# Accumulating transfers inside the product sums of a spectral filter, with finer loads and a new order

## The chip, the cores and the metric

One core of one Trainium2 chip runs the whole program. The metric is the device time of one execution in microseconds (us). Times inside the program are counted from the start of the profiled span.

## The reference

Two layers, the same twice; x is 2048 tokens by 448 features in bf16:

```python
def _A_ref(x, w_r, w_i):                     # W has 2048 x 225 entries
    X = rfft2(x.astype(float32), axes=(-2, -1)) * (w_r + 1j * w_i)
    return irfft2(X, s=(2048, 448), axes=(-2, -1)).astype(bfloat16)

def _B_ref(x, w1, b1, w2, b2):               # 448 -> 1792 -> 448
    h = relu(x @ w1 + b1)
    return (h * h) @ w2 + b2

x = x + _A_ref(_layernorm(x), A_w_r, A_w_i)
x = x + _B_ref(_layernorm(x), B_w1, B_b1, B_w2, B_b2)
x = x + _A_ref(_layernorm(x), A_w_r, A_w_i)
x = x + _B_ref(_layernorm(x), B_w1, B_b1, B_w2, B_b2)
```

## The kernel before

All stages keep their data in SBUF. Tokens lie as 16 tiles of 128 (xin for the input, x_sb for the running sum). A layer has these stages:

- **A** (A1 in layer 1, A2 in layer 2, mixed into the end of layer 1's FFN): layer norm statistics and the first short transform over tokens, 16 tiles, to XA.
- **spectral** (line 1140): for each of the items, a pair p of frequency groups (1 to 7, and 0 for the two groups that stand alone), **TD** (line 809, the transform over features, two halves a pair, each with an evacuation to U), **B** (line 820, the second transform over tokens with the matrices G, evacuated to EF), **W** (line 861, the filter) on VectorE, and **Bi** (line 903, the inverse with H or HS), evacuated to VT.
- **TI, AI** (lines 937 to 1001): the inverse transforms over features and tokens, added to x_sb; **ln** (line 1018): the second layer norm and a transposed copy yT.
- **h, o** (lines 1058 to 1122): the FFN.

W works on pairs (2,3), (4,5), (6,7) two at a time, and on 1 and 0 alone. For a pair it takes E and F (in layer 1, except pair 1, first their sum T0 and T1), multiplies them with the filter rows and their mirror image (two products, T2 to T5), and then goes one of two ways. For pairs 4 to 7 (the tuple SUMS) two sums give Z and Bi sums the rest itself, with four matmuls of 512 columns a half. For pairs 1 to 3 two sums give T6 and T7 and two more give Z, and Bi takes four matmuls of 256 columns a half. With `n=2` a sum has 896 elements a partition and a product 1792; with `n=1`, half of that.

Filter rows come from DRAM to Wt. Their mirror image (token frequency -k) is gathered by GpSimd to Wm, which lies in the memory of yT, and copied reversed from there to Wt by two transfers on SP's queue.

The order of all work is written out. Each instruction is first recorded with its dependences (from the memory it reads and writes), grouped in units that carry a tag; the table ORDER gives a rank to each unit of a tag, with a letter where the engine is chosen (a ScalarE, d VectorE, p GpSimd) and after a colon its PSUM banks. `ranked` and `schedule` (lines 392 and 413) sort all units by rank; each engine and each DMA queue then runs its own in that order, and waits only on semaphores. A DMA also waits until the one 20 places ahead of it on SP's queue is through. WARM puts matmuls without use at the start. The numbers in `cost` and `lat` are the planner's and do nothing on the chip.

## Time and profile before

| what | us |
|---|---|
| median of 3 runs (266.8 to 268.77) | 267.41 |
| the profiled execution | 267.51 |
| its span, first to last instruction | 265.7 |
| TensorE busy with matmuls | 256.0 |
| VectorE busy | 211.5 |
| ScalarE busy | 171.7 |
| GpSimd busy | 9.9 |

The profile is one execution. Its own time and its span differ by 1.8 us that lie before the first and after the last instruction. A busy TensorE may still be waiting between matmuls, since these are pipelined and their ends are modelled: where a rate matters, starts of rows are compared. The granted TensorE clock is 1.0 of full speed throughout.

### The profile page before, as it was taken

To read this page: it belongs to the slowest core of one execution; us is meant where nothing else is said; L and a number is where in the kernel's file an instruction comes from. 1 tells how busy PE (TensorE), PEld (TensorE's weight loads), DVE (VectorE), ACT (ScalarE), POOL (GpSimd) and SP (SyncE) were. 2 spreads that over 40 slices of the span, in tenths; PEclk is the share of its full clock that TensorE was granted. 3 is DMA by queue.
4 is the path that set the end of the run, shared out by engine and by line. 5 is a ranking of instruction groups with operands and counts; after the bars stand their busy time and mean duration, and the time that the engine had idled before them with its cause. 6 is when DMAs were issued, how large, how long until landed. Compare 5 with 4: busy or idle time off the path is not lost. (4 is left out here: it accounts for less than half of the span.)

```text
span 265.7 us, 5784 instructions
## 1 busy us (share of the span) xinstructions
PE 256.0 (96%) x2188; PEld 161.6 (61%) x2190; DVE 211.5 (80%) x646; ACT 171.7 (65%) x392; POOL 9.9 (4%) x30
## 2 busy tenths in 40 slices
...
GB/s 235 273 318 209 158 293 220 2 39 42 75 2 0 41 73 62 20 0 0 2 0 4 2 2 0 2 41 4 41 74 42 0 57 133 53 4 0 72 39 48
DMA packets 29423, 17.82 MB, mean 67 GB/s; under 512 B 22066, under 2 KB 28306, under 8 KB 29268
## 3 DMA queue, kind: packets, MB, share of 16 engines
...
q10 hardware_dynamic: 432, 0.69, 0.8%
...
q14 instruction: 10, 0.08, 0.1%
...
## 5 line engine op out<-in xcount | busy, mean ns | idle before, releaser
L556 PE MATMUL ps<-yT,W_sb 64*128 64x512 bf16 (+1 forms) x770 | 90.2, 346 | 0.0
L556 PE MATMUL ps<-W_sb,arena 128*128 128x448 bf16 (+2 forms) x490 | 87.3, 336 | 0.0
L556 PEld LDWEIGHTS ps<-yT,W_sb 64*128 64x128 bf16 (+1 forms) x770 | 55.0, 95 | 32.0 <-issue 1.5
L556 PEld LDWEIGHTS ps<-W_sb,arena 128*128 128x128 bf16 x490 | 46.2, 98 | 36.6 <-DVE arena L608 0.9
L575 ACT ACTIVATE arena<-ps,b1col 128x512 bf16<-128x512 f32 x84 | 51.8, 692 | 14.6 <-PE ps L556 14.5
L608 DVE TENSOR_TENSOR arena<-arena 128x512 bf16<-128x512 bf16 (+1 forms) x140 | 45.2, 369 | 17.2 <-ACT arena L575 16.8
L581 ACT ACTIVATE arena<-ps 128x448 bf16<-128x448 f32 (+1 forms) x42 | 24.5, 686 | 3.5 <-PE ps L556 3.4
L1120 DVE SCALAR_TENSOR_TENSOR x_sb<-ps,arena 128x448 bf16<-128x448 f32 (+2 forms) x27 | 15.2, 570 | 14.4 <-PE ps L556 14.3
L1024 ACT ACTIVATE VT<-x_sb 128x448 bf16<-128x448 bf16 x32 | 18.5, 581 | 12.3 <-DVE x_sb L1000 12.3
L575 ACT ACTIVATE arena<-ps 128x256 bf16<-128x256 f32 x56 | 18.0, 396 | 6.3 <-PE ps L556 6.2
L575 ACT ACTIVATE mv<-mv,epst 128x1 f32<-128x1 f32 (+1 forms) x45 | 12.6, 296 | 14.2 <-DVE rstd L715 7.3
L581 ACT ACTIVATE VT<-ps 128x512 bf16<-128x512 f32 (+1 forms) x28 | 13.9, 578 | 6.7 <-PE ps L556 6.6
L556 PE MATMUL ps<-yT,VT 64*128 64x512 bf16 x42 | 15.8, 376 | 0.0
L581 ACT ACTIVATE XA<-ps 128x512 bf16<-128x512 f32 x27 | 14.5, 593 | 1.0 <-PE ps L556 1.0
L556 PE MATMUL ps<-HS_sb,arena 128*128 128x512 bf16 x62 | 14.7, 380 | 0.2
L556 PE MATMUL ps<-arena,G_sb 128*128 128x448 bf16 (+1 forms) x76 | 14.4, 333 | 0.1
L556 PE MATMUL ps<-TD_sb,XA 112*64 112x112 bf16 (+2 forms) x312 | 13.4, 224 | 0.0
L556 PEld LDWEIGHTS ps<-TD_sb,XA 112*64 112x64 bf16 (+2 forms) x312 | 12.1, 108 | 1.3 <-issue 0.4
L608 DVE TENSOR_TENSOR tmp<-arena,Wt 128x896 bf16<-128x896 bf16 (+1 forms) x14 | 10.9, 820 | 1.9 <-DMA Wt<-yT 1.8
L592 ACT ACTIVATE arena<-x_sb,rstd 128x448 bf16<-128x448 bf16 x10 | 6.6, 667 | 8.9 <-DMA yT<-arena 4.6
L556 PE MATMUL ps<-x_sb,xin 128*128 128x256 bf16 x64 | 8.9, 272 | 3.1 <-ACT x_sb L592 1.8
L1050 DVE SCALAR_TENSOR_TENSOR arena<-x_sb,mv,b2row 128x448 bf16<-128x448 bf16 x16 | 10.7, 681 | 0.1
...
## 6 DMA issues: line engine op xcount, KB each, us to landing
...
G_sb<-c_G SPq DMA_DIRECT2D x1, 960.0 KB, 7.9
xin<-in_A_x_dram SPq DMA_DIRECT2D x4, 224.0 KB
Wt<-yT SPq DMA_DIRECT2D x2, 392.0 KB, 8.7
xin<-in_A_x_dram ACTq DMA_DIRECT2D x3, 224.0 KB, 3.3
```

The costliest lines, as they stand in the source:

```text
L556: return sch.add("pe", lambda e: e.matmul(_res(o), lhsT, rhs, start=start, stop=stop, skip_group_check=skip), [lhsT, rhs], [o], cost=cost, ...
L575: sch.add("act", lambda e: e.activation(o, _res(i), func, **kw), rd, [o], cost=c)
L581: op = sch.add(engs[0], lambda e: e.activation(o, _res(i), ACT.Copy) if h[0].eng == "act" else e.tensor_copy(o, _res(i)), [i], [o], cost=c ...
L592: op = sch.add(engs[0], lambda e: e.activation(o, i, ACT.Copy, scale=s) if h[0].eng == "act" else e.tensor_scalar(o, i, s, 1.0, op0=ALU.mu ...
L608: sch.add(eng, lambda e: e.tensor_tensor(o, _res(a), b, op), [a, b], [o], cost=_free(o) / rate + 69.0)
L1024: sch.add("act", lambda e, i=i, o=o, x=x: e.activation(o, x, ACT.Square, accum_out=mv[:, i, 4:5]), [x], [o, mv[:, i, 4:5]], cost=560.0)
L1050: small(lambda e, o=o, x=x, m=m: e.scalar_tensor_tensor(out=o, in0=x, scalar=m, in1=b2row[:], op0=ALU.add, op1=ALU.add), [x, m, b2row[:]], ...
L1120: small(lambda e: e.scalar_tensor_tensor(out=o, in0=_res(i), scalar=r[0] if r else 1.0, in1=xb[:, t, d0:d1], op0=ALU.mult, op1=ALU.add), [ ...
```

## The change

- The last two sums of pairs 2 and 3 (in both layers) and of pair 1 (in layer 2) are no longer formed from T6 and T7: a transfer from SBUF to SBUF, issued by GpSimd, adds products T4, T5 onto T2, T3 (`dma_add`). One product is made with negated filter rows so that the difference is a sum; GpSimd or ScalarE negates them once a layer, into W2_sb (layer 1) or xin (layer 2). Two sums on VectorE (tag V) then give Z.
- Pairs 4 and 5 go the same way, and so leave SUMS: Bi takes matmuls of 256 columns for them. Pairs 6 and 7 stay.
- The products get two or three scratch areas: tmp, tmp2 (in yT, over Wm), and tmp3 (in xin).
- Filter, G and W2 are loaded in more pieces and in another order, from input tile 5 instead of 7 on; W2's first nine blocks come after layer 1's filter. J is loaded late.
- b1 is loaded in rows and turned by a matmul with J.
- ORDER is new throughout, and layer 2 takes its pairs in the order 6, 7, 2, 3, 4, 5, 1, 0. There are 15 matmuls of WARM instead of 12.

The core of the diff; of ORDER only the new lines that are spoken of:

```diff
--- before.py
+++ after.py
...
-SUMS = {True: (4, 5, 6, 7), False: (4, 5, 6, 7)}
+ADDS = {True: (2, 4), False: (1, 2, 4)}
+ADD_LAT = 4500.0
+ITEMS = {True: (1, 2, 3, 4, 5, 6, 7, 0), False: (6, 7, 2, 3, 4, 5, 1, 0)}
+SUMS = {True: (6, 7), False: (6, 7)}
...
+    "dve.arena": "28", "sp.TD_sb": "54", "sp.G_sb": "21 25 18 24",
+    "sp.Wt": "22 26 19 16 73 61 69 60 20 17 71 62 23 51", "sp.H_sb": "211 200", "sp.HS_sb": "182", "sp.TI_sb": "70",
+    "sp.J_sb": "253", "sp.FI_sb": "196", "sp.b2row": "241", "sp.b1in": "166", "b1": "286:6 290d",
+    "sp.W1_sb": "218 207 234 262", "sp.W2_sb": "156 276", "A1.0": "29 30 34 35 31p 67p 81:2 108a",
+    "A1.14": "97 110 98 103 112 120 111p 121p 138:5 154a 122a 141:7 146d", "NA1": "171p 184p 213p 223p",
+    "TD0.1": "153:6 172d 161:0 169a", "B0.1": "185:6 193a 189:0 197a", "W0.1": "195 205 206 209 228 231",
+    "B0.3": "168:4 178d", "W0.3": "180 181 186 190 194", "V0.3": "242 244", "TD0.4": "177:7 183a 176:3 187a",
+    "W0.5": "212 210 225 217 227", "V0.5": "263 261", "TD0.6": "219:2 220a 221:1 224a", "B0.6": "229:4 230a",
+    "TD0.7": "204:0 216a 214:3 215a", "B0.7": "222:6 226a", "W0.7": "236 239 250 246 255 257", "TD0.0": "232:2 233a",
+    "B0.0": "237:6 243a", "W0.0": "267 269 272 273", "Bi0.1": "238:1 251a 235:0 240a",
+    "W1.7": "901 906 916 910", "TD1.2": "875:4 878a 903:2 904a", "B1.2": "912:3 918a 909:2 913a",
+    "TD1.3": "895:4 899d 897:5 902a", "B1.3": "905:0 911a", "W1.3": "925 919 931", "V1.3": "954 957",
+    "B1.5": "915:4 921a", "W1.5": "930 932 938", "V1.5": "963 964", "TD1.1": "882:4 891d 927:7 928a",
+    "B1.1": "929:6 935d 933:7 936a", "W1.1": "939 937 942", "V1.1": "969 970", "TD1.0": "924:0 934a",
+    "B1.0": "940:4 943a", "W1.0": "950 945 951 948", "Bi1.6": "949:3 955a 947:2 978d",
...
-WARM = {46: ((7, 512), (7, 512), (7, 512), (7, 512), (7, 512), (7, 512), (7, 512), (7, 512), (7, 512), (7, 512), (7,
-    512), (7, 512))}
+WARM = {64: ((7, 512), (7, 512), (7, 512), (7, 512), (7, 512), (7, 512), (7, 512), (7, 512), (7, 512), (7, 512), (7,
+    512), (7, 512), (7, 512), (7, 512), (7, 512))}
...
-        xin = sb("xin", [P, NT, D])
+        xw = sb("xw", [P, NT * D + 32 * LW + FB * D])
+        xin = xw[:, 0:NT * D].rearrange("p (t d) -> p t d", t=NT)
+        Wt = xw[:, NT * D:NT * D + 32 * LW].rearrange("p (q l) -> p q l", q=32)
+        W2_sb = xw[:, NT * D + 32 * LW:].rearrange("p (f d) -> p f d", f=FB)
...
-        Wt = sb("Wt", [P, 32, LW])
+        tmp2 = yT[:].rearrange("p a b c -> p (a b c)")[:, 0:8 * 4 * LW].rearrange("p (a b c d) -> p a b c d", a=8, b=2, c=2)
+        tmp3 = xin[:, 9:15, :].rearrange("p a (b c d) -> p a b c d", b=1, c=2)
...
+        def dma_add(o, i):
+            sch.add("pool", lambda e: e.dma_start(o, i, accum_op=ALU.add), [o, i], [o], is_dma=True, cost=1000.0, lat=ADD_LAT)
...
-        for i in range(2):
-            dma("sp", Wp[:, :, 3 - 2 * i, :], Wm[:, i, :].rearrange("p (k l) -> p k l", k=7)[:, ::-1, 1:225])
         memset(Z[:, :, LW:256], 0.0)
-        x4 = [xin[:, 7, :]]
-        dma("sp", J_sb[:], dc["J"], after=x4)
+        x4 = [xin[:, 5, :]]
+        w_dram = [w.rearrange("(p k) l -> p k l", k=16) for w in (A_w_r, A_w_i)]
+
+        def load_W(p0, p1):
+            for i in range(2):
+                tagged("sp.Wt", "sp", Wp[:, p0 - 1:p1 - 1, 2 * i, :], w_dram[i][:, p0:p1, 1:225], after=x4)
+
+        def mirror_W(p0, p1):
+            for i in range(2):
+                m = Wm[:, i, :].rearrange("p (k l) -> p k l", k=7)[:, ::-1, 1:225]
+                tagged("sp.Wt", "sp", Wp[:, p0 - 1:p1 - 1, 3 - 2 * i, :], m[:, p0 - 1:p1 - 1])
+
+        def load_G(c0, c1):
+            dma("sp", G_sb[:, c0:c1], dc["G"][:, c0:c1], after=x4)
+
         dma("sp", TD_sb[:], dc["TD"], after=x4)
-
-        w_dram = [w.rearrange("(p k) l -> p k l", k=16) for w in (A_w_r, A_w_i)]
-        dma("sp", G_sb[:, 6:], dc["G"][:, 6:], after=x4)
-        for i in range(2):
-            dma("sp", Wp[:, :, 2 * i, :], w_dram[i][:, 1:8, 1:225], after=x4)
+        load_G(6, 12)
+        load_W(1, 2)
+        load_G(12, 20)
+        load_W(2, 4)
+        mirror_W(1, 2)
+        load_G(20, cst["G"].shape[1])
+        mirror_W(2, 4)
+        load_W(4, 8)
+        mirror_W(4, 8)
         if H_PAIRS:
             dma("sp", H_sb[:, 2:], dc["H"][:, 2:], after=x4)
+        load_G(0, 6)
+        for i in range(2):
+            tagged("sp.Wt", "sp", W08[:, :, i, :], w_dram[i][:, 0:9:8, 1:225], after=x4)
+        dma("sp", H_sb[:, 0:2], dc["H"][:, 0:2], after=x4)
         dma("sp", HS_sb[:], dc["HS"][:, SD_PAIRS[0] - 1:SD_PAIRS[-1]], after=x4)
-        dma("sp", G_sb[:, 0:6], dc["G"][:, 0:6], after=x4)
-        dma("sp", H_sb[:, 0:2], dc["H"][:, 0:2], after=x4)
-        for i in range(2):
-            dma("sp", W08[:, :, i, :], w_dram[i][:, 0:9:8, 1:225], after=x4)
         dma("sp", TI_sb[:], dc["TI"], after=x4)
+        dma("sp", J_sb[:], dc["J"], after=x4)
         dma("sp", FI_sb[:], dc["FI"], after=x4)
         dma("sp", b2row[:], B_b2.partition_broadcast(P), after=x4)
-        dma("sp", b1in[:, 0:FB], B_b1.rearrange("(fb fl) -> fl fb", fl=P), after=x4)
-        cp(b1col[:, 0:FB], b1in[:, 0:FB])
+        dma("sp", b1in[0:FB, :], B_b1.rearrange("(fb fl) -> fb fl", fl=P), after=x4)
+        sch.tag = "b1"
+        q = _Tile(1)
+        mm(q[lambda b: ps[:, b, 0:FB]], b1in[0:FB, :], J_sb[0:FB, P - 1:P - FB - 1:-1], True, True)
+        evac(b1col[:, 0:FB], q[lambda b: ps[:, b, 0:FB]])
+        sch.tag = ""
         dma("sp", W1_sb[:, 0:3, :], B_w1[0:384, :].rearrange("(b p) f -> p b f", p=P), after=x4)
         dma("sp", W1_sb[0:64, 3, :], B_w1[384:448, :], after=x4)
-        dma("sp", W2_sb[:], B_w2.rearrange("(fb fl) d -> fl fb d", fl=P), after=x4)
-
+        w2 = B_w2.rearrange("(fb fl) d -> fl fb d", fl=P)
+        tagged("sp.W2_sb", "sp", W2_sb[:, 9:], w2[:, 9:], after=x4)
         for r in (64, 65):
             dma("sp", W1_sb[r:r + 1, 3, :], B_b1.rearrange("(o f) -> o f", o=1), after=x4)
...
+        def negate(first):
+            sch.tag = "NA1" if first else "NA2"
+            for p0 in ADDS[first]:
+                for q in range(p0 - 1, p0 + (p0 > 1)):
+                    o, i = (W2_sb if first else xin)[:, 2 * q, :], Wp[:, q, 0:2, :].rearrange("p s l -> p (s l)")
+                    negate_one(o, i)
+
+        def negate_one(o, i):
+            h = []
+            op = sch.add("pool", lambda e: e.activation(o, i, ACT.Copy, scale=-1.0) if h[0].eng == "act" else
+                         e.tensor_scalar(o, i, -1.0, 1.0, op0=ALU.mult, op1=ALU.mult), [i], [o], cost=640.0)
+            h.append(op)
+            op.alt = {"pool": 640.0, "act": 470.0}
+
         def stage_W(p0, n, first):
             z_ = Z[:, :, 0:LW]
             if p0 > 0:
                 ef = EF[:, 2 * p0:2 * (p0 + n), :].rearrange("p (q e) (r l) -> p q e r l", e=2, r=2)
                 E, F = ef[:, :, 0], ef[:, :, 1]
-                T = [tmp[:, i, 0:n] for i in range(8)]
+                tm = (tmp2 if p0 in (2, 6) else tmp) if first else {6: tmp, 2: tmp2, 4: tmp, 1: tmp3}[p0]
+                T = [tm[:, i, 0:n] for i in range(6 if tm is tmp3 else 8)]
                 w = Wp[:, p0 - 1:p0 - 1 + n].rearrange("p q (a r) l -> p a q (r l)", a=2)
                 if p0 in (VB_PAIRS if first else V_PAIRS):
                     T[0:2] = E, F
                 else:
                     tt(T[0], E, F[:, :, ::-1, :], ALU.subtract)
                     tt(T[1], E[:, :, ::-1, :], F, ALU.add)
-                for i, wi in enumerate((w, w[:, ::-1])):
+                add = p0 in ADDS[first]
+                w0 = w
+                if add:
+                    x = (W2_sb if first else xin)[:, 2 * (p0 - 1):2 * (p0 + n) - 3:2, :]
+                    w0 = bass.AP(x.tensor, x.offset, [list(x.ap[0]), [w[:, 1].offset - x.offset, 2], [4 * LW, n], [1, 2 * LW]])
+                for i, wi in enumerate((w0, w[:, ::-1])):
                     t = T[i].rearrange("p q r l -> p q (r l)")[:, None].to_broadcast([P, 2, n, 2 * LW])
-                    tt(tmp[:, 2 + i:5 + i:2, 0:n].rearrange("p a q r l -> p a q (r l)"), t, wi, ALU.mult)
+                    tt(tm[:, 2 + 2 * i:4 + 2 * i, 0:n].rearrange("p a q r l -> p a q (r l)"), t, wi, ALU.mult)
                 z = z_[:, 4 * p0:4 * (p0 + n), :].rearrange("p (q s) l -> p q s l", s=4)
+                k = 2
+                if add:
+                    a, b = [tm[:, j:j + 2, 0:n].rearrange("p a q r l -> p a (q r l)") for j in (2, 4)]
+                    dma_add(a, b)
+                    sch.tag = sch.tag.replace("W", "V")
+                elif p0 in SUMS[first]:
+                    tt(z[:, :, 0:2], T[4], T[2], ALU.subtract)
+                    tt(z[:, :, 2:4], T[3], T[5], ALU.add)
+                    return
+                else:
+                    tt(T[6], T[4], T[2], ALU.subtract)
+                    tt(T[7], T[3], T[5], ALU.add)
+                    k = 6
                 if p0 in SUMS[first]:
-                    tt(z[:, :, 0:2], T[3], T[2], ALU.subtract)
-                    tt(z[:, :, 2:4], T[4], T[5], ALU.add)
-                    return
-                tt(T[6], T[3], T[2], ALU.subtract)
-                tt(T[7], T[4], T[5], ALU.add)
+                    raise ValueError
                 def both(r):
-                    b, c = T[6][:, :, r], T[7][:, :, 1 - r]
+                    b, c = T[k][:, :, r], T[k + 1][:, :, 1 - r]
                     p_, q_, l_ = [list(x) for x in b.ap]
                     return bass.AP(b.tensor, b.offset, [p_, [c.offset - b.offset, 2], q_, l_])
                 tt(z[:, :, 0:2].rearrange("p q a l -> p a q l"), both(1), both(0), ALU.subtract)
                 zz = z[:, :, 3:1:-1].rearrange("p q a l -> p a q l")
-                t = tmp[:, 6:8, 0:n]
+                t = tm[:, k:k + 2, 0:n]
                 tt(zz, t[:, :, :, 0], t[:, :, :, 1], ALU.add)
...
-            items = (1, 2, 3, 4, 5, 6, 7, 0)
+            items = ITEMS[first]
             def rank(k, n):
                 sch.tag = f"{k}{L}.{n}"
+            negate(first)
             for n, p in enumerate(items):
-                rank("TD", n)
+                rank("TD", p)
                 stage_TD(p, first)
-                rank("B", n)
+                rank("B", p)
                 stage_B(p, first)
-                rank("W", n)
+                rank("W", p)
                 if p in (1, 3, 5, 7):
                     stage_W(max(p - 1, 1), min(p, 2), first)
                 elif p == 0:
                     stage_W(0, 1, first)
+            if first:
+                tagged("sp.W2_sb", "sp", W2_sb[:, 0:9], w2[:, 0:9], after=x4)
             for n, p in enumerate(items):
-                rank("Bi", n)
+                rank("Bi", p)
                 stage_Bi(p, first)
         def ffn(last):
```

## Rows read from the trace of the kernel before

**Rows 1.** The page: span, and busy time of each engine.

```profile
span 265.7 us, 5784 instructions
...
PE 256.0 (96%) x2188; PEld 161.6 (61%) x2190; DVE 211.5 (80%) x646; ACT 171.7 (65%) x392; POOL 9.9 (4%) x30
```

**Rows 2.** The chain of waits, in order of time: start, us, what.

```profile
172.84 90.34 PE ps L556 x700
```

**Rows 3.** TensorE's timeline, layer 1: start, us, instruction, idle before it and releaser.

```profile
17.31 2.46 PE L556 MATMUL ps<-TD_sb,XA 128*128 128x224 bf16 x24
...
33.27 2.14 PE L556 MATMUL ps<-H_sb,arena 128*128 128x256 bf16 x18 [1.14 <-DVE arena L608]
...
43.52 2.26 PE L556 MATMUL ps<-TI_sb,VT 112*128 112x224 bf16 x24
```

**Rows 4.** TensorE's timeline, layer 2.

```profile
145.06 2.55 PE L556 MATMUL ps<-TD_sb,XA 112*64 112x112 bf16 x96
...
166.98 2.09 PE L556 MATMUL ps<-TI_sb,VT 112*128 112x224 bf16 x24
...
173.01 3.22 PE L556 MATMUL ps<-yT,W_sb 128*128 128x256 bf16 x28
...
176.07 0.56 PE L556 MATMUL ps<-TI_sb,VT 112*128 112x112 bf16 x8
```

**Rows 5.** VectorE's timeline, layer 1.

```profile
22.96 1.16 DVE L608 TENSOR_TENSOR tmp<-arena,Wt 128x896 bf16<-128x896 bf16 x2 [1.77 <-DMA Wt<-yT]
...
28.91 1.16 DVE L608 TENSOR_TENSOR tmp<-tmp 128x896 bf16<-128x896 bf16 x2
...
29.99 1.16 DVE L608 TENSOR_TENSOR tmp<-arena 128x896 bf16<-128x896 bf16 x2
...
36.27 2.10 DVE L608 TENSOR_TENSOR tmp<-tmp,Wt 128x1792 bf16<-128x1792 bf16 x2
...
38.40 1.16 DVE L608 TENSOR_TENSOR arena<-tmp 128x896 bf16<-128x896 bf16 x2
...
41.15 0.69 DVE L582 CAST VT<-ps 128x512 bf16<-128x512 f32 x1
```

**Rows 6.** VectorE's timeline, layer 2.

```profile
148.79 1.16 DVE L608 TENSOR_TENSOR tmp<-arena,Wt 128x896 bf16<-128x896 bf16 x2
...
164.33 0.69 DVE L608 TENSOR_TENSOR arena<-tmp 128x448 bf16<-128x448 bf16 x2
...
164.94 2.54 DVE L582 CAST VT<-ps 128x512 bf16<-128x512 f32 x5
```

**Rows 7.** DMA issues: queue, kind, count, KB each, median us to landing.

```profile
Wt<-yT SPq DMA_DIRECT2D x2, 392.0 KB, 8.7
...
Wt<-in_A_w_i_dram SPq DMA_DIRECT2D x1, 392.0 KB, 5.6
...
G_sb<-c_G SPq DMA_DIRECT2D x1, 960.0 KB, 7.9
...
TD_sb<-c_TD SPq DMA_DIRECT2D x1, 224.0 KB, 4.3
...
TD_sb<-c_TQ SPq DMA_DIRECT2D x1, 196.0 KB, 2.7
...
yT<-in_A_w_r_dram,back POOLq DMA_INDIRECT x1, 4.8
```

**Rows 8.** Busy time in stretches; the last columns are DMA share and GB/s.

```profile
14.00:16.00 2.00, 2.00 (x20) 1.78 (x19) 1.85 (x8) 2.00 (x7) 1.56 (x5) 1.00 1.01 371
...
18.00:20.00 2.00, 2.00 (x22) 1.80 (x20) 1.44 (x3) 1.45 (x4) 0.00 (x0) 1.00 1.19 266
```

**Rows 9.** Groups of GpSimd's instructions: count, busy us, mean ns, idle before.

```profile
L593 POOL TENSOR_SCALAR x_sb<-FA_sb,rstd 128x256 bf16<-128x256 bf16 x12 | 5.7, 485 | 1.3 <-DVE rstd L715 1.1
```

**Rows 10.** SP's timeline: the first issues after the input.

```profile
7.33 0.67 SPq L548 DMA_DIRECT2D Wt<-in_A_w_r_dram  x1
...
8.70 0.60 SPq L548 DMA_DIRECT2D TD_sb<-c_TD  x1
```

23 lines of the change are left out of this document (18 added, 5 removed), and 180 rows, old and new, of the table ORDER.

## The prediction

> **What bounds the kernel now.** The page gives the span and TensorE's busy share [rows 1]; it is high everywhere, so I asked where the end is decided. The chain of waits says it: from 172.84 us on, TensorE runs 90 us without waiting [rows 2]. Nothing in the change shortens that stretch. Time can only come from before it, and the FFN of layer 1 is full in the same way. That leaves the two spectral filters, from the first TD matmul, or from the last matmul of the second layer norm, to the first TI matmul.
>
> Layer 1, TensorE's timeline [rows 3]: TD starts at 17.31, TI at 43.52, 26.2 us later, and one Bi matmul stands 1.14 us idle until a VectorE product is there. Layer 2 [rows 4]: 145.06 to 166.98, 21.9 us, and hardly idle. A 256-column matmul costs 0.109 us there (28 in 3.06 us, from 173.01 to 176.07), so 512 columns cost about 0.217.
>
> VectorE's timelines show the other engine of this stretch. In layer 1 [rows 5] it stands 1.77 us idle until 22.96, when the mirrored filter has landed, and then has no gap worth the name until 41.15, when the last sums are done and a cast begins; TI follows 2.37 us later. In layer 2 [rows 6] its products run from 148.79 to 164.94, TI 2.04 us later. So both engines are nearly full, and VectorE's last sum releases the last Bi matmuls: the price of a VectorE instruction on that row counts, while TensorE's saving counts only as far as VectorE gets done sooner.
>
> Prices on VectorE, start to start: a sum of 896 elements 0.54 us (28.91 to 29.99 for two), a product of 1792 1.07 us (36.27 to 38.40 for two) [rows 5], a sum of 448 0.31 us (164.33 to 164.94 for two) [rows 6]. An 896 product goes as 0.54, a cast of 448 or 512 as 0.6.
>
> **What is taken away.** Pairs 4 and 5 leave the form in which Bi does the last sums (4 matmuls of 512 columns a half) for the form of pairs 1 to 3 (4 of 256): 16 matmuls a layer cheaper by 0.108, so TensorE saves 1.73 us a layer. VectorE loses two sums of 896 for pairs 2 and 3 (1.08 us a layer) and, in layer 2, two of 448 for pair 1 (0.62): 1.08 and 1.70 us. For pairs 4 and 5 its count does not change: their two final sums now read what the transfer added. The 2-byte load of b1 and one small copy go too, a matmul and a small evacuation come; all small.
>
> **What is added: the transfers.** Two in layer 1, three in layer 2, issued by GpSimd after a pair's second product; the pair's last sums wait for them on VectorE, in order, with everything behind. What hides one is the VectorE work that stands between, by the new order: in layer 1 for pairs 2 and 3, four instructions of pair 1 (1.70), pairs 4 and 5 up to their products (3.22), pair 1's last sums (0.62) and two sums (1.08): 6.6 us. For pairs 4 and 5: 0.62, 1.08, 1.08, two products (2.14), 1.08: 6.0 us. In layer 2 for pairs 2 and 3: two products 2.14, a cast 0.57, pair 1's products 1.08, pair 0 1.70: 5.5 us; for pairs 4 and 5, and for pair 1, 4.8 us each.
>
> No row shows an accumulating transfer. Bounds for 448 KB from issue to landing, from [rows 7]: below, a copy on empty engines: the 196 KB load of the tables took 2.7 us, of which at 371 GB/s [rows 8] 0.54 are bytes, so 2.2 + 459 KB/371 = 3.4 us. Above, the 392 KB mirror copy from SBUF to SBUF beside all other loads, 8.7 us. In between, the GpSimd gather of about 400 KB beside the loads, 4.8 us. I take 5.0 in layer 2, where nothing else moves, and 6.0 in layer 1, nearest to the gather and stretched for the loads: stalls of 0.2 and 0 us. The Trainium skill ("Collectives: The Full Stack", the section on the bandwidth ceiling) says that a reducing transfer reads two sources for each write, so that its read side carries twice the bytes. By that, the copy of 3.4 us would be 2.2 + 2.5 = 4.7 us, still just under 4.8; no run here shows it.
>
> GpSimd also negates filter rows: four instructions in layer 1. The nearest row is its 256-element scaling, 485 ns [rows 9], so about 0.85 for 448 elements as an upper bound. Two run before the products, two between the transfers; cover is the 6 us above. In layer 2 they lie in the FFN, where TensorE is full.
>
> **What is moved: loads.** The filter goes in 12 pieces instead of 4, G in 4 instead of 2, W2 in 2 instead of 1: 11 more issues on SP at about 0.6 us [rows 10]. They now start when token tile 5 is there instead of tile 7; in before the first issue after the input stands at 7.33 [rows 10]. TD, which TensorE needs at 17.31, was third in that list (8.70, landed 4.3 later, [rows 7]); now 784 KB of the filter and 1,152 KB of G stand ahead of it, 1.98 MB. At 371 GB/s these take 5.3 us, at 266 GB/s [rows 8] 7.4 us: TD lands at 18.3 to 20.4, less about 1.8 us for the earlier start, so 16.5 to 18.6, that is 0 to 1.3 us late. I take 0.3, as the later bytes of both orders are nearly the same. The mirrored pieces come in time for their products, but not all for something else: the first two results of pairs 2 and 3 go to the new scratch over the gathered filter, so they wait until every mirror copy has read it. In before the last of these landed at 22.96 [rows 5]. Ahead of it now stand the rest of G and TI, 0.4 MB or 1.1 to 1.5 us, against 1.8 of earlier start and no 2-byte load in the rings: 22.3, between 21.5 and 23.5. The reverse matrix J now stands behind W1 and b2, and a matmul that reads it stands in TensorE's queue just before TI; I take it as in time.
>
> **The sum.** Layer 1: the first filter sums of pairs 2 and 3 need six half transforms (24 matmuls, 2.4 us as in the first line of [rows 3]), their B (8 of 448 columns at 0.19, 1.5) and an evacuation (about 0.7), so TensorE lets them start at 21.9 and the mirror copies at 22.3, instead of 22.96: -0.7. Two sums less: -1.08. A cast now stands ahead of the last sums: +0.6. After the last sum TensorE has 8 matmuls of 256 and 4 of 512, 1.74 us instead of 2.37: -0.6. Gaps between a product and the sum that reads it: -0.2. TD late: +0.3. Together -1.7.
> Layer 2: four sums less, -1.70. Seven casts instead of six stand before the first product, and the last of them waits for pair 3's transform behind the B of pairs 6 and 7: the start moves from 3.7 to about 4.7 us after the last layer-norm matmul, +1.0. Three casts among the sums (1.47) instead of one (0.6): +0.9. The gaps (16.15 us measured against 15.4 by the prices) shrink by 0.5. After the last sum 12 matmuls of 256 and a wait, 1.5 instead of 2.04: -0.5. Transfers +0.2. Together -0.6.
> The profiled execution took 267.5 us; 267.5 - 2.3 = 265.2. It lies 0.1 above the median of the runs, so **265.1 us**.
>
> **Rivals.**
> *The transfers are late.* If they take 8.7 us like the mirror copy, VectorE stalls 8.7 - 6.6 = 2.1 and then 0.6 us in layer 1, 3.2 and 0.7 in layer 2: 6.6 us, of which 0.2 is in the sum: 265.1 + 6.4 = 271.5, slower than before. For it speaks that the loads fill the DMA engines in layer 1; against it, that in layer 2 they are empty. It decides from about 6.6 us a transfer, where the stalls (0 and 0.6 in layer 1, 1.1 and 0.7 in layer 2) eat the gain.
> *VectorE stops being the bound.* If the casts and gaps that I charged fall into waits anyway, TensorE's need sets the end: layer 1 less the 1.1 idle and 1.73, layer 2 less 1.73 and 0.4 (one more half transform is done before the last layer-norm matmul): 267.4 - 5.0 = 262.4. For it: in layer 2 TensorE has hardly a gap [rows 4].
> *Loads eat layer 1's gain.* TD 1.3 us late and the last mirror copy at 23.5 instead of 22.3 add 1.0 and, beyond that, 0.8: 265.1 + 1.8 = 266.9. For it: TD's new place; against it: the earlier start.
> *GpSimd holds VectorE up.* If the two negations between the transfers each stop a VectorE sum for 0.85 us, layer 1 loses 1.7: 266.8. No row of before has GpSimd busy beside a two-input VectorE instruction. The Trainium skill ("SBUF — State Buffer", "Who interferes with whom") says that just this pair, a VectorE instruction with two SBUF inputs and a GpSimd one that reads SBUF, excludes one another; no run here shows it yet.
>
> **Chances.** Forecast 0.48, with 263.6 to 266.6 as its own range; TensorE as the bound 0.15; loads 0.14; GpSimd 0.08; late transfers 0.15, of which some end between 266 and 270. About 1% (2.7 us) is what a measurement of this kernel can tell from no change, so faster means under 264.8: nearly half of the forecast (0.22), the second case (0.15) and the lighter part of the loads and GpSimd cases (0.05), 0.42; same 0.45; slower 0.13. The range of 8 in 10 is 262.2 to 268.8.
>
> **What would show it.** Of the 32 matmuls with HS a layer, 16 have 256 columns instead of 512. TI's first matmul at 41.8 in layer 1 (43.5 before), and in layer 2 21.3 us after the last layer-norm matmul (21.9). VectorE's idle time before the last sums put down to the GpSimd transfer: near 0. TD's first matmul no later than 17.6, and no wait of TensorE for J. If TI moves by 2 us and the time does not, the gain was given back in the transition to the FFN, which I take as unchanged; that would prove me wrong, as would transfers over 6.6 us.

## The result: 1.3% slower

The changed kernel took 270.6 us (median), the kernel before 266.7 beside it on the same chip: a ratio of 1.013, with a 95% interval from 1.009 to 1.017. The forecast was 265.1 in a range from 262.2 to 268.8. The first profile of the changed kernel, on which the expectations of the first four runs rest, was of a disturbed execution (span 275.8 us), so every row of after below is from a second profile of the same kernel, the run `again`.

The page of after:

```profile
span 269.5 us, 5807 instructions
PE 255.6 (95%) x2192; PEld 164.4 (61%) x2194; DVE 215.5 (80%) x647; ACT 171.3 (64%) x389; POOL 18.0 (7%) x40
...
PE   8769959999999999999999999999999999999996
DVE  5975999799797999879989899899994894265532
...
PEclk9999999999999999999999999999999999999999
DMA  7999983020322032200000008002230223300012
```

TensorE's busy time is almost what it was (255.6 us, 256.0 before [rows 1]), the span 3.8 us longer. Both profiled executions (271.48 and 267.51 us) lie about 0.8 us above the medians, so these 3.8 us stand for the 3.9 of the medians. A slice is 6.7 us: TensorE's 6 in the third and 5 in the sixth slice lie between 13 and 40 us, in the filter of layer 1, and the DMA engines stand at 9 tenths from the second slice to the fifth.

TensorE's timeline in layer 1 (start, duration, what, count; in brackets the idle time before and what ended it):

```profile
20.54 2.46 PE L579 MATMUL ps<-TD_sb,XA 128*128 128x224 bf16 x24 [2.91 <-DMA TD_sb<-c_TD]
...
40.90 4.62 PE L579 MATMUL ps<-HS_sb,arena 128*128 128x512 bf16 x27 [1.03 <-DVE arena L631]
...
47.30 2.10 PE L579 MATMUL ps<-TI_sb,VT 112*128 112x224 bf16 x24
```

TD starts at 20.54 instead of 17.31, after 2.91 us without work, and TI at 47.30 instead of 43.52 [rows 3]. VectorE in the same stretch, and GpSimd below it:

```profile
25.34 1.16 DVE L631 TENSOR_TENSOR yT<-arena 128x896 bf16<-128x896 bf16 x2 [0.46 <-ACT arena L604]
...
29.61 2.19 DVE L631 TENSOR_TENSOR tmp<-tmp 128x448 bf16<-128x448 bf16 x2
...
36.95 1.16 DVE L631 TENSOR_TENSOR arena<-yT 128x896 bf16<-128x896 bf16 x2 [0.40 <-DMA yT<-yT]
...
44.04 0.68 DVE L631 TENSOR_TENSOR arena<-tmp 128x448 bf16<-128x448 bf16 x2
44.64 0.68 DVE L605 CAST VT<-ps 128x512 bf16<-128x512 f32 x1
```

```profile
20.84 1.10 POOL L919 TENSOR_SCALAR xw<-xw 128x448 bf16<-128x448 bf16 x2 [5.12 <-DMA xw<-yT]
29.12 0.99 POOL L573 DMA_DIRECT2D yT<-yT  x1 [7.19 <-DVE tmp L631]
29.79 1.47 POOL L919 TENSOR_SCALAR xw<-xw 128x448 bf16<-128x448 bf16 x2
35.18 0.89 POOL L573 DMA_DIRECT2D tmp<-tmp  x1 [3.93 <-DVE arena L631]
```

VectorE's filter work starts at 25.34 instead of 22.96 [rows 5]. From 29.61 on, two sums of 448 take 2.19 us, where two such rows otherwise take 0.68 (44.04), and just then GpSimd runs its last two negations (29.79, 1.47 us; the first two, at 20.84, took 1.10). At 36.95 the sums of pairs 2 and 3 have waited 0.40 us for the transfer issued at 29.12.

Layer 2, TensorE:

```profile
147.01 1.76 PE L579 MATMUL ps<-TD_sb,XA 112*64 112x112 bf16 x64
...
149.58 1.86 PE L579 MATMUL ps<-TD_sb,XA 112*64 112x112 bf16 x64
...
170.57 2.10 PE L579 MATMUL ps<-TI_sb,VT 112*128 112x224 bf16 x24
```

From the last layer-norm matmul (149.58) to TI 20.99 us, 21.92 before [rows 4]. The 3.8 us divide by the starts of these rows so:

| stretch | before | after | difference |
|---|---|---|---|
| start to VectorE's first filter instruction, layer 1 | 22.96 | 25.34 | +2.38 |
| from there to the cast behind the last sums | 18.19 | 19.30 | +1.11 |
| from that cast to TI | 2.37 | 2.66 | +0.29 |
| TI to the last layer-norm matmul of the transition | 101.54 | 102.28 | +0.74 |
| from there to TI of layer 2 | 21.92 | 20.99 | -0.93 |
| TI to the end | 98.72 | 98.93 | +0.21 |
| sum (the span) | 265.7 | 269.5 | +3.8 |

Layer 1 loses 3.78 us. Layer 2's filter, from the last layer-norm matmul to TI, is 0.93 us shorter, but the stretch ahead of it and the one behind it are together 0.95 longer, so the span keeps nothing of that.

### The profile page after: what moved, and what is told of

Its sections match the earlier page's. It is cut to its first block, busy times and chain, and to the rows that moved or that the text cites. A ratio compares the mean times of both kernels' runs of the same rounds, so it can differ in the third digit from the quotient of the medians.

```text
span 275.8 us, 5807 instructions
## 1 busy us (share of the span) xinstructions
PE 258.6 (94%) x2192; PEld 164.4 (60%) x2194; DVE 215.4 (78%) x647; ACT 171.6 (62%) x389; POOL 18.0 (7%) x40
## 3 DMA queue, kind: packets, MB, share of 16 engines
q1 hardware_dynamic: 27456, 15.97, 21.3%
HBM read 11.15 MB, written 1.84 MB: 47 GB/s over the span
## 4 chain that ended last, share of the span: by engine, by line
PE 80%; DMA 7%; ACT 5%; SPq 3%; DVE 3%; issue 1%
PE ps L579 80%; ACT arena L604 4%; DMA tmp<-tmp 3%; SPq L568 3%; DMA TD_sb<-c_TD 2%; DMA xw<-in_A_x_dram 2%; DVE tmp L631 1%; ACT tmp L604 1%; DVE yT L605 1%; DVE tmp L605 0%; DVE arena L631 0%; DVE VT L631 0%; DVE x_sb L631 0%; DVE x_sb L635 0%; DVE x_sb L1197 0%
## 5 line engine op out<-in xcount | busy, mean ns | idle before, releaser
L579 PE MATMUL ps<-xw,arena 128*128 128x448 bf16 (+2 forms) x490 | 87.6, 336 | 0.0
L579 PEld LDWEIGHTS ps<-xw,arena 128*128 128x128 bf16 x490 | 46.2, 98 | 36.7 <-DVE arena L631 0.7
L604 ACT ACTIVATE arena<-ps 128x448 bf16<-128x448 f32 (+1 forms) x41 | 23.7, 668 | 9.1 <-PE ps L579 8.9
L604 ACT ACTIVATE VT<-ps 128x512 bf16<-128x512 f32 (+1 forms) x25 | 12.5, 567 | 12.8 <-PE ps L579 12.7
L579 PE MATMUL ps<-TD_sb,XA 112*64 112x112 bf16 (+2 forms) x312 | 15.3, 231 | 2.7 <-DMA TD_sb<-c_TD 2.7
L579 PE MATMUL ps<-HS_sb,arena 128*128 128x256 bf16 (+1 forms) x62 | 12.8, 355 | 4.8 <-DVE arena L631 4.6
L579 PEld LDWEIGHTS ps<-HS_sb,arena 128*128 128x128 bf16 x64 | 6.5, 105 | 9.4 <-DVE arena L631 5.8
L605 DVE CAST arena<-ps 128x448 bf16<-128x448 f32 (+1 forms) x11 | 6.8, 660 | 6.4 <-PE ps L579 6.4
L1077 DVE SCALAR_TENSOR_TENSOR x_sb<-ps,mv,xw 128x448 bf16<-128x448 f32 x16 | 10.7, 680 | 1.0 <-PE ps L579 0.8
L604 ACT ACTIVATE tmp<-ps 128x896 bf16<-128x896 f32 (+1 forms) x14 | 10.6, 814 | 1.2 <-PE ps L579 1.2
```

Source lines behind the costliest of these rows:

```text
L579: return sch.add("pe", lambda e: e.matmul(_res(o), lhsT, rhs, start=start, stop=stop, skip_group_check=skip), [lhsT, rhs], [o], cost=cost, ...
L604: op = sch.add(engs[0], lambda e: e.activation(o, _res(i), ACT.Copy) if h[0].eng == "act" else e.tensor_copy(o, _res(i)), [i], [o], cost=c ...
L605: e.tensor_copy(o, _res(i)), [i], [o], cost=c[engs[0]], unit=unit)
L1077: small(lambda e, xx=xx, xi=xi, r=r, m=m: e.scalar_tensor_tensor(out=xx, in0=_res(r), scalar=m, in1=xi, op0=ALU.subtract, op1=ALU.add), [r ...
```

## The experiments

Theory: layer 1 loses in three places, TD's late landing, the negations beside VectorE's sums, and an accumulating transfer that is late because loads run beside it. Four runs (`td`, `neg`, `w2`, `late`) each change one of these alone; then come pairs and all three, the transfers taken out of one layer at a time, and one attempt at something better. All runs but `again` and `w2` write some ranks as decimal fractions, for which `ranked` takes `float(w)` instead of `int(w)`; that alone changes nothing in the order. In the table "queue" is the issue of SP's first load behind the input (it waits for input tile 5, in the kernel before for tile 7), "first sum" is VectorE's first filter instruction of layer 1, "transfer" the first accumulating one (issue, time to landing, VectorE's wait for it), TI the first TI matmul of layer 1; all from the profiles, in us.

| run | edit | queue | first sum | transfer | TI | span | median | ratio to before, 95% interval |
|---|---|---|---|---|---|---|---|---|
| before | | 7.33 | 22.96 | | 43.52 | 265.7 | 266.7 | |
| again | none | 6.73 | 25.34 | 29.12, 7.8, 0.40 | 47.30 | 269.5 | 271.31 | 1.016, 1.007 to 1.025 |
| td | TD early | 5.96 | 22.32 | 26.39, 8.9, 1.54 | 45.69 | 267.9 | 269.83 | 1.013, 1.006 to 1.020 |
| neg | negations early | 5.79 | 23.23 | 27.01, 8.4, 2.50 | 45.77 | 268.0 | 270.49 | 1.016, 1.009 to 1.022 |
| w2 | last W2 load late | 6.56 | 26.39 | 30.17, 6.6, 0 | 47.86 | 270.1 | 272.17 | 1.020, 1.012 to 1.028 |
| late | W1, W2 loads late | 5.66 | 23.59 | 27.4, 4.4, 0 | 45.06 | 267.3 | 269.11 | 1.011, 1.006 to 1.016 |
| tdneg | TD, negations | 6.88 | 23.37 | 27.2, 9.5, 3.59 | 47.02 | 269.2 | 270.16 | 1.013, 1.008 to 1.018 |
| tdlate | TD, loads | 5.60 | 22.29 | 26.7, 4.4, 0 | 44.47 | 266.7 | 268.46 | 1.007, 1.003 to 1.010 |
| tdneglate | all three | 6.92 | 23.02 | 26.8, 4.4, 0 | 42.98 | 265.2 | 266.42 | 1.001, 0.999 to 1.003 |
| noadd1 | TD, no transfers in layer 1 | 5.68 | 22.49 | none | 44.95 | 267.4 | 268.94 | 1.010, 1.007 to 1.013 |
| noadd1late | the same, loads late | 5.67 | 22.35 | none | 44.81 | 267.1 | 269.25 | 1.011, 1.007 to 1.015 |
| noadd2 | TD, no transfers in layer 2 | 5.62 | 22.28 | 26.1, 9.2, 1.84 | 45.67 | 270.5 | 272.71 | 1.027, 1.020 to 1.034 |
| best | all three, scratch exchanged | 5.53 | 22.71 | 26.5, 4.4, 0 | 42.72 | 264.9 | 266.51 | 1.000, 0.998 to 1.003 |

### again: the changed kernel once more

No edit.

> The changed kernel itself, unaltered, for a profile to set beside the one of before. Theory: what it loses lies in layer 1 alone and in three places: TensorE waits 2.5 to 3 us for TD after the input's transform, VectorE loses 1.3 to 1.6 us beside two negations on GpSimd, and it waits 3.5 to 4 us for the second accumulating transfer (issue to landing 9 to 10 us). Sum 7.3 to 8.6 us, less what layer 1 saves elsewhere; the first TI matmul of layer 1 comes about 4 us later than the 43.52 us of before, and layer 2 gets about 0.9 us shorter up to its TI. Rival: the waits shrink in a second profile, and the 3.5 us are spread over layers 1 and 2 without one place. Time about 270.3 us by both.

Measured: 271.31 us. TD's 2.91 us and VectorE's 1.5 came as expected. The wait for the second transfer did not: it landed in 5.3 us and nothing waited. It was the first transfer, with 7.8 us, that was late, by 0.40. So the first two places stood, and the third had to be looked for anew.

### td: TD's load early

```diff
-"sp.TD_sb": "54"
+"sp.TD_sb": "18.5"
```

> Only TD's load moves, from 13th to 4th behind the input. Theory (the wait for TD is on the path): TensorE starts TD's matmuls at 17.6 instead of 20.3 us, VectorE's first sums come 1.5 to 2.7 us earlier, and so does all that follows: 267.6 to 268.8 us. Rival (the wait is hidden by the mirror copies of the filter, which land near 25 us and which the products of pairs 2 and 3 need anyway): VectorE then idles before its first sums on a transfer, the sums still start near 26 us, and the time stays at 269.8 to 270.4 us.

```profile
17.51 2.46 PE L579 MATMUL ps<-TD_sb,XA 128*128 128x224 bf16 x24
```

```profile
22.32 1.26 DVE L631 TENSOR_TENSOR yT<-arena 128x896 bf16<-128x896 bf16 x2 [0.46 <-ACT arena L604]
...
35.35 1.16 DVE L631 TENSOR_TENSOR arena<-yT 128x896 bf16<-128x896 bf16 x2 [1.54 <-DMA yT<-yT]
```

The first fence is TensorE, the second VectorE. TD's wait is gone, and the first sums come at 22.32, 3.0 us earlier (part of it by the queue's earlier start, 5.96 against 6.73): the mirror copies were no obstacle here, and the rival falls. But TI gained only 1.61 of the 3.0 (45.69); of the rest, 1.14 stand at 35.35, where the wait for the first transfer rose from 0.40 to 1.54. 269.83 us is above the expected 267.6 to 268.8: the wait was on the path, but half of it came out again behind the transfer.

### neg: the negations ahead of the first transfer

```diff
-"NA1": "171p 184p 213p 223p"
+"NA1": "171p 184p 184.3p 184.6p"
```

> The last two negations of layer 1 stay on GpSimd but come ahead of the first accumulating transfer's issue instead of behind it, so that they run while VectorE casts out of PSUM or idles. Theory (a sum of two SBUF inputs stands still while GpSimd negates): the pair of 128x448 sums that took 2.19 us takes about 0.7 again, the second transfer is issued about 1.5 us earlier, and the time falls by 1.0 to 1.5 us, to 268.8 to 269.3. Rival (the second transfer's landing is set by the loads beside it and not by its issue): the sums get their 0.7 us but the wait for the transfer grows by as much, and the time stays within 0.4 us of 270.3.

```profile
27.50 0.69 DVE L631 TENSOR_TENSOR tmp<-tmp 128x448 bf16<-128x448 bf16 x2
...
35.43 1.16 DVE L631 TENSOR_TENSOR arena<-yT 128x896 bf16<-128x896 bf16 x2 [2.50 <-DMA yT<-yT]
```

The two sums take 0.69 us again instead of 2.19. And the wait for the transfer is 2.50 instead of 0.40, so the rival was right about the time (270.49), with the first transfer where it named the second. TensorE waited only 0.79 us here ahead of TD's matmuls, for an evacuation, and TI stands at 45.77: the first load behind the input was issued at 5.79 instead of 6.73, and TD at 12.48 instead of 14.25, though the edit touches neither. In the profiles of the changed kernels that first load is issued between 5.53 and 6.92 us, whatever the edit, and TD, the mirror copies and the weights stand behind it in the queue. Differences in TI of a microsecond between single profiles are to be read with that in mind.

### w2: the last W2 load late

```diff
-tagged("sp.W2_sb", "sp", W2_sb[:, 0:9], w2[:, 0:9], after=x4)
+tagged("sp.W2_sb", "sp", W2_sb[:, 0:9], w2[:, 0:9], after=x4 + [b1col[:, 0:FB]])
```

> Only the last load of layer 1, 1008 KB of W2, is held back until the b1 column is there (about 53 us), so that nothing large moves beside the second accumulating transfer. Theory (W2's load, issued 0.1 us ahead of it, slows it): issue to landing falls from 9.5 to 6 to 7 us, VectorE's wait from 3.8 to 0.5 to 1.3, and the time by 2.5 to 3.3 us, to 267.0 to 267.8. Rival (the transfer of 448 KB takes its 9 us by itself, or behind what was queued before): landing stays at 8.5 us or more, and the time within 0.5 us of 270.3.

The transfers' rows of the DMA issues from 24 to 46 us (KB each, us to landing), first `again`, then `w2`:

```profile
yT<-yT POOLq DMA_DIRECT2D x1, 448.0 KB, 7.8
tmp<-tmp POOLq DMA_DIRECT2D x1, 448.0 KB, 5.3
```

```profile
yT<-yT POOLq DMA_DIRECT2D x1, 448.0 KB, 6.6
tmp<-tmp POOLq DMA_DIRECT2D x1, 448.0 KB, 4.9
```

The second transfer's wait was 0 with W2's load beside it (5.3 us) and 0 without (4.9): nothing to gain there, and theory and rival both fell with the row they were made for. The time, 272.17, is no lower. What did show is the clock, in the stretch behind TD's wait in this run (start and end, length, busy time of PE, PEld, DVE, ACT, POOL, granted clock, DMA share, GB/s):

```profile
19.90:25.40 5.50, 5.48 (x32) 4.01 (x33) 1.71 (x3) 2.13 (x5) 1.10 (x2) 0.69 1.06 337
```

After 2.22 us of waiting for TD, TensorE was granted 0.69 on the mean of the next 5.5 us (0.50, the lower of its two levels, from 21 to 24 us). Its 24 TD matmuls took 3.82 us instead of 2.46, and from their start to VectorE's first sum 6.47 us passed instead of 4.80. In `again` it waited 2.91 us, was granted 1.00, and the 24 took 2.46. So such a wait can cost 1.7 us more than its length. The granted clock of whole executions fits: three of the four of `w2` had a mean of 0.993 or 0.994 and took 272.06 to 272.58 us, the one at 1.00 took 270.35.

### tdneg: both of the first two

> TD's load early and the two negations ahead of the first accumulating transfer. Both were tried alone: each brought VectorE's products forward, and in each the first transfer, issued at 26.4 and 27.0 us, landed at 35.3 and 35.4 all the same. Theory (the transfer lands when the loads beside it, 1344 KB of W1 above all, are through): issued near 26.4, it lands at 34.5 to 35.4 again, VectorE waits 2.5 to 3.5 us for it, the first TI matmul comes at 44.8 to 45.7, and the time is 269.2 to 269.9 us, that is no more than 0.6 below TD alone. Rival (the two gains add up): the wait stays at 1.5, TI comes at 44.2, the time is 268.3.

```profile
31.93 1.15 DVE L631 TENSOR_TENSOR yT<-arena 128x896 bf16<-128x896 bf16 x2
36.67 1.16 DVE L631 TENSOR_TENSOR arena<-yT 128x896 bf16<-128x896 bf16 x2 [3.59 <-DMA yT<-yT]
```

```profile
W_sb<-in_B_w_dram SPq DMA_DIRECT2D x1, 1344.0 KB, 15.6
yT<-yT POOLq DMA_DIRECT2D x1, 448.0 KB, 9.5
tmp<-tmp POOLq DMA_DIRECT2D x1, 448.0 KB, 8.5
H_sb<-c_H SPq DMA_DIRECT2D x1, 384.0 KB, 9.8
```

The two gains do not add up: none of the four executions came under 269.3 us, where the rival had 268.3. VectorE is ready for the sums at 33.08 and waits 3.59 us: the transfer lands 9.5 us after its issue at 27.2, at 36.7. TI at 47.02 is later than either text had it, but this profile is of the slowest of the four (271.22 us), and its queue began at 6.88; the two shortest took 269.3 and 269.7 us, as the theory had it.

Across `again`, `td`, `neg`, `tdneg`, `w2` and `noadd2` the transfer is issued between 26.1 and 30.2 and lands between 35.3 and 36.9. A landing that does not follow its issue points to what runs beside it, though not to the end of W1 alone: its 1344 KB were through between 34.3 (`w2`) and 36.5 (`td`) in the five others, but here, after 15.6 us, only at 40.8. H came so late here (9.8 us) that TensorE waited 3.08 us for it as well.

### tdneglate: all three

The three loads move into `spectral` and wait for a sum of pair 5; by their ranks W1's two stand ahead of W2's last load and W2's 560 KB behind it (the edits of `td` and `neg` are left out here):

```diff
-dma("sp", W1_sb[:, 0:3, :], B_w1[0:384, :].rearrange("(b p) f -> p b f", p=P), after=x4)
-dma("sp", W1_sb[0:64, 3, :], B_w1[384:448, :], after=x4)
-tagged("sp.W2_sb", "sp", W2_sb[:, 9:], w2[:, 9:], after=x4)
...
+v5 = [Z[:, 20, 0:LW]]
+tagged("sp.W1_sb", "sp", W1_sb[:, 0:3, :], B_w1[0:384, :].rearrange("(b p) f -> p b f", p=P), after=v5)
+tagged("sp.W1_sb", "sp", W1_sb[0:64, 3, :], B_w1[384:448, :], after=v5)
+tagged("sp.W2_sb", "sp", W2_sb[:, 9:], w2[:, 9:], after=v5)
...
-"sp.W1_sb": "218 207 234 262", "sp.W2_sb": "156 276"
+"sp.W1_sb": "234 262 275.3 275.6", "sp.W2_sb": "276.5 276"
```

> The same with the loads that layer 1's filter does not need (W1's 1344 and 224 KB, W2's 560 KB) held back until the last sums of pairs 4 and 5 are done. Theory (the loads slow the transfers): the first transfer lands in 4.5 to 5.5 us as in layer 2, VectorE has no wait for it, the first TI matmul comes at 42.2 to 43.0 us, before 43.52, and the time falls to 266.4 to 267.4 us. Rival (the transfers need 7 to 9 us in this stretch by themselves, or behind the loads that are left): the wait stays over 1.5 us, TI comes after 44.2, the time is over 268.3. Second rival: W1 now comes late for the first matmuls on W, near 49 us, and TensorE waits there.

```profile
W_sb<-in_B_w_dram SPq DMA_DIRECT2D x1, 1344.0 KB, 6.3
...
yT<-yT POOLq DMA_DIRECT2D x1, 448.0 KB, 4.4
tmp<-tmp POOLq DMA_DIRECT2D x1, 448.0 KB, 4.8
```

```profile
23.02 1.16 DVE L631 TENSOR_TENSOR yT<-arena 128x896 bf16<-128x896 bf16 x2 [1.09 <-DMA xw<-yT]
...
32.64 1.15 DVE L631 TENSOR_TENSOR arena<-yT 128x896 bf16<-128x896 bf16 x2
```

```profile
42.98 2.10 PE L579 MATMUL ps<-TI_sb,VT 112*128 112x224 bf16 x24
```

The transfers take 4.4 and 4.8 us, the sums of pairs 2 and 3 follow at 32.64 without a wait, and TI comes at 42.98, 0.54 before that of the kernel before. 266.42 us is within the expectation, and TensorE does not wait for W1. VectorE's first sum, though, waited 1.09 us for the mirror copies, with the queue begun at 6.92. The three edits take the whole loss back; they do not make the kernel faster than before (ratio 1.001).

### late and tdlate: the loads alone, and without the negations

`late` has the load edit alone, `tdlate` that and TD's rank.

> Only the loads of W1 and of W2's 560 KB are held back until the last sums of pairs 4 and 5; TD late and the negations beside the sums as in the changed kernel. Theory (the three losses stand in a row, and with TD late the first transfer waits only 0.4 us for the loads): both transfers land in 4.3 to 5 us, the wait of 0.4 us goes, TD is still late by 2 to 3 us and VectorE still loses 1.5 us beside the negations; the first TI matmul comes at 46.3 to 47.0 us and the time is 269.8 to 270.8. Rival (the loads are the one cause, of TD's lateness too): TI comes before 44.5, the time is under 268.

> TD early and the same loads held back, but the last two negations where the changed kernel has them, behind the first accumulating transfer and beside VectorE's sums. Theory: nothing but those negations now separates it from the run with all three edits, so the pair of 128x448 sums takes 2.19 us instead of 0.69, TI comes 1.5 us behind that run's 42.98, at 44.3 to 44.7, and the time is 267.6 to 268.2. Rival (VectorE's 1.5 us are hidden behind TensorE or a transfer): within 0.4 us of that run's 266.4.

TensorE's first TD matmuls in `late`, then VectorE's sums beside the negations in `tdlate`:

```profile
18.79 2.46 PE L579 MATMUL ps<-TD_sb,XA 128*128 128x224 bf16 x24 [1.04 <-DMA TD_sb<-c_TD]
```

```profile
27.23 2.19 DVE L631 TENSOR_TENSOR tmp<-tmp 128x448 bf16<-128x448 bf16 x2
```

`late` came out better than expected (45.06 and 269.11 against 46.3 to 47.0 and 269.8 to 270.8): TD was 1.04 us late in this profile, not 2 to 3, with its issue at 12.5 us as in `neg`. The loads held back have no part in that: the queue began at 5.66 instead of 6.73, and the twelve loads ahead of TD are the same in both; W1 is issued 9 us behind TD in `again`. The loads are not the one cause: VectorE still loses its 1.5 us, and the time is 2.7 us above the run with all three.
`tdlate` settled the negations: 44.47 against 42.98, 1.49 us, just what the pair of sums takes more. In time it is 2.0 (268.46 against 266.42), somewhat over the expected 268.2. Against `td`, from which it differs by the loads alone and which has the same first sum (22.32, 22.29), the first transfer takes 4.4 us instead of 8.9, the wait of 1.54 us is gone, and TI comes 1.22 us earlier: this pair shows that the loads delay the transfer.

### noadd1 and noadd1late: layer 1 without transfers

```diff
-ADDS = {True: (2, 4), False: (1, 2, 4)}
+ADDS = {True: (), False: (1, 2, 4)}
...
-"W0.3": "180 181 186 190 194", "V0.3": "242 244"
+"W0.3": "180 181 186 190 194 194.5 242 244"
...
-"W0.5": "212 210 225 217 227", "V0.5": "263 261"
+"W0.5": "212 210 225 217 231.1 231.2 263 261"
```

Both have TD early, and NA1 is gone; `noadd1late` also has the load edit.

> TD's load early, and layer 1 without accumulating transfers and negations: its four product sums of pairs 2 to 5 are on VectorE again (four instructions of 0.58 us, 2.3 us), layer 2 keeps its transfers. Theory (in layer 1 the transfers give back all they save: 1.5 us beside the negations and 1.5 for the first transfer): TI comes at 44.8 to 45.2 us instead of TD's 45.69, the time is 268.7 to 269.4, no worse than with the transfers. Rival (the transfers do pay in layer 1): TI at 46.5 or later, 270.6 us or more.

> TD early, the same loads held back, and no accumulating transfers in layer 1: its four sums and no negations, on VectorE. It is the pair to the run with all three edits, which differs by the transfers alone. Theory (without transfers the loads slow nothing that is on the path): the first TI matmul stays at 44.6 to 45.1 us, the time at 268.6 to 269.2, and the transfers are worth 2.0 to 2.6 us in layer 1 once they are not disturbed. Rival (the held-back loads help by themselves, through H and HS): TI at 43.5 to 44.2, the time near 267.5.

TensorE in `noadd1` and in `noadd1late`:

```profile
44.95 2.10 PE L579 MATMUL ps<-TI_sb,VT 112*128 112x224 bf16 x24
```

```profile
44.81 2.10 PE L579 MATMUL ps<-TI_sb,VT 112*128 112x224 bf16 x24
```

With the loads as changed, doing without transfers is 0.74 us earlier at TI than `td` with them, and 0.9 us in time. The intervals of the two ratios overlap and the queues began 0.28 us apart, so this shows only that in that surrounding the transfers save nothing. Holding the loads back does nothing for a layer 1 without transfers (44.81 against 44.95; 269.25 against 268.94), so in these two no load delayed H, HS or anything else on the path. And `noadd1late` against `tdneglate` gives what the transfers and their negations save in layer 1: 1.83 us at TI, and 2.50 from the first sum to TI (22.46 against 19.96), for `tdneglate`'s queue began 1.25 us later and its first sum came 0.67 later; 2.8 in time. The expected 2.0 to 2.6 us lie between these.

### noadd2: layer 2 without transfers

```diff
-ADDS = {True: (2, 4), False: (1, 2, 4)}
+ADDS = {True: (2, 4), False: ()}
...
-"W1.3": "925 919 931", "V1.3": "954 957"
+"W1.3": "925 919 931 931.5 954 957"
...
-tt(T[6], T[4], T[2], ALU.subtract)
-tt(T[7], T[3], T[5], ALU.add)
-k = 6
+k = 0 if tm is tmp3 else 6
+if k == 0:
+    T[0:2] = [tm[:, i, 0:n] for i in range(2)]
+tt(T[k], T[4], T[2], ALU.subtract)
+tt(T[k + 1], T[3], T[5], ALU.add)
```

W1.5 and W1.1 get one more sum likewise, and NA2 is gone; pair 1, whose scratch has no places 6 and 7, uses its first two. TD is early.

> TD's load early, layer 1 as changed, but layer 2 without accumulating transfers and negations: its product sums of pairs 1 to 5 are on VectorE again (six instructions, about 2.9 us). Theory (in layer 2 the transfers land in 4.5 us with nothing beside them, nothing waits for them, and VectorE's sums lie on the path): the stretch from the last W2 matmul to the first TI matmul of layer 2, 24.3 us with the transfers, gets 1.2 to 2.6 us longer, and the time is 271.0 to 272.4. Rival (TensorE is the bound there, and VectorE's sums are hidden): under 0.6 us longer, 269.8 to 270.4.

TensorE in layer 2, `noadd2`, then `td`:

```profile
145.13 1.76 PE L579 MATMUL ps<-TD_sb,XA 112*64 112x112 bf16 x64
...
171.60 2.10 PE L579 MATMUL ps<-TI_sb,VT 112*128 112x224 bf16 x24
```

```profile
145.43 1.76 PE L579 MATMUL ps<-TD_sb,XA 112*64 112x112 bf16 x64
...
168.99 2.10 PE L579 MATMUL ps<-TI_sb,VT 112*128 112x224 bf16 x24
```

From the first TD to TI 26.47 us without the transfers, 23.56 with them: 2.91 us, a little over the upper end expected, and as much as the six sums cost by the expectation. So in layer 2 VectorE's sums lie on the path to the last, and the transfers, which land in 4.3 to 4.5 us there, hide completely:

```profile
yT<-yT POOLq DMA_DIRECT2D x1, 448.0 KB, 4.3
tmp<-tmp POOLq DMA_DIRECT2D x1, 448.0 KB, 4.5
xw<-xw POOLq DMA_DIRECT2D x1, 224.0 KB, 4.5
```

(the DMA issues of layer 2 in `again`).

Neither price is one against the kernel before. Without the transfers pairs 4 and 5 need four sums, where the kernel before, with Bi's matmuls of 512 columns, gave them two: 1.08 us a layer at its prices. Against the kernel before, the new form with its transfers gains 0.54 us up to TI in layer 1 when all is mended (`tdneglate`), and 0.37 in layer 2 from its first TD to TI.

### best: scratch tiles exchanged

```diff
-tm = (tmp2 if p0 in (2, 6) else tmp) if first else {6: tmp, 2: tmp2, 4: tmp, 1: tmp3}[p0]
+tm = (tmp if p0 in (2, 6) else tmp2) if first else {6: tmp, 2: tmp2, 4: tmp, 1: tmp3}[p0]
...
-T = [tmp[:, i] for i in range(2)]
+T = [(tmp2 if first else tmp)[:, i] for i in range(2)]
```

on top of all three edits.

> The run with all three edits, and the two scratch tiles of layer 1 exchanged: pairs 2 and 3 work in the tile of their own, and pairs 1, 4, 5 and 0 in the one that lies over the gathered filter, so that VectorE's first sums no longer wait for the last mirror copies to be read out of it. Theory: VectorE's first sums start at 22.3 to 22.5 us instead of 23.02, the first TI matmul comes at 42.2 to 42.6, and the time is 265.6 to 266.2 us, 0.2 to 0.6 below the run with all three edits. Rival (the mirror copies are needed 2 us later anyway, or TensorE's Bi stage is the bound): TI at 42.9 or later, 266.4 us.

TensorE:

```profile
42.72 2.10 PE L579 MATMUL ps<-TI_sb,VT 112*128 112x224 bf16 x24
```

The wait for the mirror copies is gone (1.09 us before the first sum in `tdneglate`, now 0.40 for an evacuation), but the queue began 1.39 us sooner here, and `td` and `noadd2`, with queues nearly as early (5.96, 5.62) and no exchange, did not wait for them either: the profiles do not show that the exchange did it. The first sum came at 22.71, not 22.3 to 22.5, and TI at 42.72, just above the expected end. The 0.3 us of the spans (264.9 against 265.2) do not show in the times (266.51 against 266.42). No version here beats the kernel before.

## Why the prediction was wrong, step by step

**What bounds the kernel** held. The FFN and the tail are unchanged to 0.2 us (98.93 against 98.72), and the kernel's time was decided ahead of them, in the two filters and the transition to layer 2's. `noadd2` speaks against the rival in which TensorE sets the end: six more sums on VectorE cost 2.91 us.

**Layer 2** held up to TI, but the span got nothing of it. Forecast were -0.6 and 21.3 us from the last layer-norm matmul; measured were 20.99, which is -0.93. Of this some is work moved ahead: 64 TD matmuls now stand between the last layer-norm matmuls and those before them, instead of 48:

```profile
143.05 1.37 PE L556 MATMUL ps<-TD_sb,XA 112*64 112x112 bf16 x48
```

(before; after, 147.01). From the first TD of layer 2 on 23.56 us stand against 23.93, a gain of 0.37; the way from layer 1's TI to there is 0.18 longer and the tail 0.21, both of which the prediction took as unchanged. The transfers were taken at 5.0 us, measured 4.3 to 4.5, and no sum waited. TensorE did not wait for J either.

**The loads: the mis-sized term is "TD late, +0.3, bounds 0 to 1.3".** TD's landing was worked out from that of before (13.0), 5.3 to 7.4 us for the bytes now ahead of it, and an earlier start of 1.8 us; 0.3 us late means 17.6. It landed at 20.25. SP's rows show why:

```profile
6.73 0.91 SPq L568 DMA_DIRECT2D xw<-in_A_w_i_dram  x2
...
14.25 0.60 SPq L568 DMA_DIRECT2D TD_sb<-c_TD  x1
...
23.52 1.21 SPq L568 DMA_DIRECT2D W_sb<-in_B_w_dram  x1
```

The first load behind the input is issued at 6.73, only 0.6 us before the 7.33 of before [rows 10], for tile 5 was not there sooner. TD, 13th in that queue, is issued 7.5 us behind it, where it was 1.4 behind [rows 10]: SP took about 0.6 us for each of the twelve before it. And it lands 6.0 us after its issue, not 4.3 [rows 7]. Ten more issues and the longer landing come to 7.85 us, above the bounds of 5.3 to 7.4 that the bytes gave. The prediction counted the eleven added issues and their 0.6 us, and did not put them in front of TD; the longer landing stood in no term.

The bound of 1.3 was passed in three profiles of five with TD in this place. TensorE waited 2.7 us for it in the first profile of the changed kernel, 2.9 in `again` and 2.2 in `w2`, but 1.0 in `late` and not at all in `neg`. The earlier start of 1.8 us nearly came in that first one, `late` and `neg` (5.66 to 5.83) and not in the other two, while the way from the first load to TD's landing, 12.4 to 14.2 us against 5.7 before, was long in all five. The start of VectorE, forecast at 22.3 with TD in time, came in `td` (22.32) and `tdlate` (22.29), so the -0.7 was there to be had; but what the first sum waited for there was an evacuation on ScalarE, forecast for 21.9, and not the mirror copies, forecast for 22.3.

**GpSimd beside VectorE: a rival with 0.08 that came true in full.** Forecast price 1.7 us, measured 1.5 in the row (2.19 against 0.69 in `neg`) and 1.49 at TI (`tdlate` against `tdneglate`). The rule of the Trainium skill ("SBUF — State Buffer", "Who interferes with whom") spoke against this step, and the trace agrees with it. I gave it 0.08 because no row of before showed such a pair; but the order of the units, which was in the diff, puts the negations behind the transfer's issue and so beside VectorE's sums without a gap, and a rule that names just this pair deserved better odds than that.

**Late transfers: right that they would be late, wrong in how that shows.** In layer 1 the first transfer, beside the loads, took 6.6 to 9.5 us, not 6.0. By the stated rule (it decides from about 6.6 us) VectorE should have waited 1.2 us for the 7.8 of `again`, and it waited 0.40. The cover was longer than the 6.6 us forecast, for a bad reason: the instructions between (issue at 29.12, sums wanted at 36.55) include the 1.5 us at which VectorE stood beside the negations. Take that away and the cover is 5.9 us (27.2 to 33.08 in `tdneg`), and the wait comes out. It falls short of the 6.6 because the transfer is issued 0.6 us behind the end of the product (28.50 to 29.12 in `again`), which the prediction left out. The copy on empty engines that served as the lower bound, 3.4 us, was passed by 0.9 us or more everywhere: 4.3 to 4.9 without loads, once 5.9 (the second one in `tdlate`). The rule on the two reads of a reducing transfer ("Collectives: The Full Stack" in the Trainium skill, on the bandwidth ceiling) had given 4.7, and that comes near. The bytes are not what sets it, though: in layer 2 the 224 KB of pair 1 took 4.5 us, as long as 448 KB.

**The rest of layer 1.** From the first sum to the cast, -1.08 + 0.6 - 0.2 = -0.68 was forecast. Measured is +1.11, less 1.5 beside the negations and 0.40 for the transfer: -0.79, as forecast. The tail is the other term that failed: -0.6 was forecast, +0.29 measured. I had TensorE finish only 8 matmuls of 256 columns and 4 of 512 behind the last sum; but the 27 matmuls of HS that start at 40.90, after 1.03 us of waiting for VectorE, run to 45.35, past the last sum's end at 44.72, and only then come those 12. This is what is left when all else is mended. In `tdneglate` layer 1 is 0.54 us shorter up to TI, not 1.7: the start stands at +0.06 (with 1.09 us of waiting for the mirror copies), the stretch to the cast at -0.89, the tail again at +0.29. Layer 2 adds 0.04, so the span is 0.5 us shorter, where the sum had -2.3.

**The chances.** Loads, negations and late transfers were priced as three rivals that exclude one another, each an unlikely single event. They all sat in one stretch of 20 us, and the reason for each (finer pieces, the order around the transfer, full DMA engines in layer 1) was there at once. All three came true, and the time, 270.6, ended near the 271.5 of the rival with the largest loss, though by another sum: 2.38 for the start, 1.50 for the negations, 0.40 for the transfer, less 0.50 for the rest.
